# The last projection in four column strips, and a block that ends without GpSimd's drain

## Chip, cores, metric

The kernel runs on one core of one Trainium2 chip. The metric is the device time of one execution in microseconds (us). Executions of one kernel here spread over 0.2 to 0.7 us of 1329, and the change edits the last three microseconds. So the document uses two rulers. The timed runs say whether the whole became faster. The trace says what each step after the last load took; those steps repeat within about 0.01 us from look to look (a look is one profiled execution).

## The reference

Two decode attentions, A and B, each with one query token and 32 query heads of 128; their two outputs of 512 stand side by side.

```python
# A: 32 key/value heads, all 32768 keys.  B: 8 key/value heads, the last 4096 keys.
q = (x @ wq).reshape(B, Sq, H, Dh).transpose(0, 2, 1, 3)
scores = jnp.einsum("bhqd,bhkd->bhqk", q, k_cache) * (Dh ** -0.5)
p = softmax(scores)
o = jnp.einsum("bhqk,bhkd->bhqd", p, v_cache)
out = o.transpose(0, 2, 1, 3).reshape(B, Sq, H * Dh) @ wo      # [1,4096] @ [4096,512]
# ... result: concatenate([out_A, out_B], -1), bfloat16 [1, 1, 1024]
```

Nearly all bytes are A's keys and values: 2 x 32 x 32768 x 128 x 2 bytes = 537 MB of the 570 MB read.

## The kernel before

The kernel streams K and V through two large buffers. After the last head the weight `wo` of A comes in five pieces (`WO_CUTS`), each with its own semaphore, so that the projection follows the pieces as they land. A row of the result is a sum over 32 matmuls with one stationary column each. To use more of the PE array than one column, each matmul is split into two strips of 256 result columns; they go to different column groups of the array and to PSUM partitions 0 and 64, and run together (the two start 3 to 4 ns apart in the trace).

```python
    def build(self):
        nc = self.nc
        with nc.Block() as block:
            # ... plan the operations of each engine, then emit them

    WO_CUTS = {"A": (0, 11, 19, 25, 29, 32), "B": (0, 16, 32)}

    def plan(self):
        # ... all loads and both attentions; the loads of wo are issued last
        self.emit_spread("A")
        self.emit_proj()
        for n in ("B", "A"):
            self.op("sp", lambda e, n=n: e.wait_ge(self.outsem[n], 16))

    def proj_part(self, name, part, out):
        a0, a1 = self.WO_CUTS[name][part:part + 2]
        # ... one matmul group for each a in a0..a1, via `out`
        return self.op("pe", mm, (self.wosem[name][part], 16), self.c[name]["ozop"])

    def halves(self, e, bank, lhsT, rhs, begin, end):
        for i in range(2):
            inst = e.matmul(bank[64 * i:64 * i + 1, 0:256], lhsT=lhsT, rhs=rhs[:, 256 * i:256 * i + 256], start=begin,
                            stop=end, tile_position=(0, 64 * i), skip_group_check=True)
        return inst

    def store(self, name, bank, off, dep):
        c = slice(off // 2, off // 2 + 256)
        o = self.op("dve", lambda v: v.tensor_copy(self.out_sb[0:65, c], bank[0:65, 0:256]), dep)
        self.op("sp", lambda e: e.dma_start(self.out[0, :, off:off + 512].rearrange("a (i x) -> (a i) x", i=2),
                                            self.out_sb[0:65:64, c]).then_inc(self.outsem[name], 16), o)

    def emit_proj(self):
        # ... B: four strips of 512 over heads, copied to pb, summed by two halves into ACC
        self.store("B", self.ACC, 512, o)
        for part in range(len(self.WO_CUTS["A"]) - 1):
            o = self.proj_part("A", part, lambda e, lhsT, rhs, a: self.halves(e, self.PT, lhsT, rhs, a == 0, a == 31))
        self.store("A", self.PT, 0, o)
```

## Time and profile before

| | |
|---|---|
| Time, median of 3 runs | 1328.72 us (1328.62 to 1329.13) |
| Span in the profile | 1326.8 us |
| DMA | 430 GB/s over the span |
| Last piece of A's `wo` landed | 1323.81 us |

In the views, PE is TensorE's matmuls, PEld its weight loads, DVE VectorE, ACT ScalarE, POOL GpSimd and SP SyncE; a q marks an instruction of the engine's instruction queue. A load or store has landed when its semaphore is full. Lines of the page of the kernel before: span, the granted PE clock and the DMA busy share in 40 slices (tenths), and the chain that ended last, by engine.

```profile
span 1326.8 us, 28797 instructions
...
PEclk9877788887788888778888878888887888888798
DMA  9999999999999999999999999999999999999998
...
DMA 70%; PE 28%; DVE 1%; issue 0%; SPq 0%; ACT 0%
```

DMA is busy nine tenths or more in 39 slices of 40, and 70% of the chain is DMA. PE's clock in these slices of 33 us is an average. A change of the projection can therefore only gain where DMA has nothing left to do: after the last load.

The same chain in order of time, its last pieces (start, length, what). The DMA piece is the last load from its issue to its landing.

```profile
1290.58 33.23 DMA kbuf<-in_A_wo_dram
...
1323.85 0.51 PE psPT L655 x6
...
1324.39 0.42 DVE out_sb L661
```

The timeline of the end, without the weight loads (start, length, engine, line, operation, count; in brackets the idle time before it and what ended it):

```profile
1323.85 0.49 PE L655 MATMUL psPT<-kbuf,oz_A 128*1 128x256 bf16 x6 [0.34 <-DMA kbuf<-in_A_wo_dram]
1324.39 0.42 DVE L661 CAST out_sb<-psPT 65x256 bf16<-65x256 f32 x1 [5.65 <-PE psPT L655]
1324.84 0.49 SPq L662 DMA_DIRECT2D out_dram<-out_sb  x1
```

After the load: PE 0.51 us, VectorE's cast 0.42 us, SyncE's store. The store's semaphore was full at 1326.34, 1.50 us after its issue began. From there to the end of the span are 0.47 us. They are the block's end; the instructions of it on SyncE, and GpSimd's drain (line 94; duration, then first and last start):

```profile
L94 POOLq DRAIN  x1: 1817/1817/1817, 1.2 to 1.2; - x1
...
L94 SPq COMPARE_BRANCH  x1: 33/33/33, 1326.4 to 1326.4; - x1
L94 SPq DRAIN  x1: 7/7/7, 1326.6 to 1326.6; - x1
L94 SPq EVENT_SEMAPHORE  x1: 17/17/17, 1326.7 to 1326.7; - x1
```

GpSimd's drain starts at 1.2 us and lasts until 3.0, while GpSimd sets up its constants. SyncE goes through a branch and a drain at the end, then a barrier of all engines. The span ends at 1326.8; the device time is longer, after the program's end.

PE's busy time, the granted clock and the DMA share in the last three windows of the trace's clock record, 3.41 us each:

```profile
core 0: us, PE busy (x) PEld busy (x) DVE busy (x) ACT busy (x) POOL busy (x), PEclk, DMA share, GB/s
1316.56:1319.98 3.42, 2.26 (x38) 1.22 (x32) 1.11 (x2) 0.00 (x0) 0.00 (x0) 1.00 0.99 401
1319.98:1323.39 3.41, 2.19 (x36) 1.19 (x32) 0.00 (x0) 0.00 (x0) 0.00 (x0) 1.00 0.44 177
1323.39:1326.80 3.41, 0.61 (x10) 0.18 (x6) 0.42 (x1) 0.00 (x0) 0.00 (x0) 1.00 0.00 0
```

The clock is full (1.00) up to the last matmul; PE was busy 2.26 and 2.19 us of 3.41 in the two windows before the last load.

### The profile page before, as it was taken

What the parts mean: (1) busy time and instruction counts of PE and PEld (TensorE: products, weight loads), DVE (VectorE), ACT (ScalarE), POOL (GpSimd) and SP (SyncE); (2) the same over time, 40 slices, a digit from 0 to 9 for tenths busy, and PEclk for the clock granted to TensorE, in tenths of its full rate; (3) what the DMA queues carried; (4) which work ended last, traced back from release to release, by engine and by line L of the source; (5) the groups of instructions that cost most, each with busy time, mean ns of one, the idle gap of its engine ahead of it and who ended that gap; (6) DMA issues with size and microseconds to landing.
All of it is one profiled execution on the core that took longest, in us unless ns stands there. A gap on an engine that the chain in (4) does not pass through costs nothing.

```text
span 1326.8 us, 28797 instructions
## 1 busy us (share of the span) xinstructions
PE 964.5 (73%) x13436; PEld 679.5 (51%) x13436; DVE 749.8 (57%) x1345; ACT 54.8 (4%) x167; POOL 2.3 (0%) x17
## 2 busy tenths in 40 slices
PE   3757678777667877766787777678777767877786
PEld 3544455554445555444565544456554445655453
DVE  3645466665456666545666645566654556665473
ACT  0000000000000000000000000000000000000000
POOL 0000000000000000000000000000000000000000
PEclk9877788887788888778888878888887888888798
DMA  9999999999999999999999999999999999999998
GB/s 394 431 431 438 432 433 433 437 429 433 433 435 437 433 435 431 433 433 435 437 433 435 431 433 433 431 441 433 431 435 433 431 433 441 433 431 435 433 431 344
DMA packets 13079, 570.66 MB, mean 430 GB/s; under 512 B 1540, under 2 KB 1544, under 8 KB 1928
## 3 DMA queue, kind: packets, MB, share of 16 engines
q1 hardware_dynamic: 12776, 570.43, 99.6%
q8 instruction: 12, 0.20, 0.1%
q10 hardware_dynamic: 288, 0.00, 0.0%
q14 instruction: 3, 0.02, 0.0%
HBM read 570.43 MB, written 0.00 MB: 430 GB/s over the span
## 4 chain that ended last, share of the span: by engine, by line
DMA 70%; PE 28%; DVE 1%; issue 0%; SPq 0%; ACT 0%
DMA kbuf<-in_A_k_cache_dram 65%; PE psT L491 23%; PE psS L513 4%; DMA kbuf<-in_B_k_cache_dram 3%; DMA kbuf<-in_A_wo_dram 3%; DVE kt L494 1%; PE psACC L593 0%; SPq L286 0%; DVE oc_A L609 0%; ACT psb L541 0%; DVE tr_in L530 0%; PE psPT L565 0%; ACT ptsb L568 0%; PE psPT L655 0%; PE psG L620 0%
## 5 line engine op out<-in xcount | busy, mean ns | idle before, releaser
L494 DVE COPY kt<-psT 128x1024 bf16<-128x1024 bf16 x1056 | 655.2, 684 | 245.0 <-PE psT L491 243.1
L491 PE MATMUL psT<-ident,kbuf 128*128 128x128 bf16 x8448 | 579.2, 234 | 176.2 <-DMA kbuf<-in_A_k_cache_dram 164.4
L491 PEld LDWEIGHTS psT<-ident,kbuf 128*128 128x128 bf16 x8448 | 539.7, 106 | 268.2 <-DMA kbuf<-in_A_k_cache_dram 172.5
L593 PE MATMUL psACC<-vbuf,ptsb 128*4 128x512 bf16 (+1 forms) x2112 | 183.2, 523 | 23.1 <-ACT ptsb L568 21.3
L513 PE MATMUL psS<-kt,qw 128*32 128x512 bf16 x2048 | 157.6, 385 | 15.5 <-DVE kt L494 15.5
L607 DVE TENSOR_SCALAR oc_A<-psACC,hot_A 128x128 f32<-128x128 f32 x32 | 11.2, 351 | 247.8 <-PE psG L620 247.8
L593 PEld LDWEIGHTS psACC<-vbuf,ptsb 128*4 128x4 bf16 (+1 forms) x2112 | 60.0, 110 | 136.9 <-issue 87.2
L541 ACT ACTIVATE psb<-psS,nb_A 128x512 bf16<-128x512 f32 x32 | 22.0, 687 | 1169.9 <-DVE nb_A L540 1169.9
L513 PEld LDWEIGHTS psS<-kt,qw 128*32 128x32 bf16 x2048 | 34.0, 95 | 58.0 <-DVE kt L494 31.4
L620 PE MATMUL psG<-oc_A,hw 128*32 128x128 f32 (+1 forms) x128 | 19.3, 227 | 52.3 <-DVE oc_A L609 52.3
L620 PEld LDWEIGHTS psG<-oc_A,hw 128*32 128x32 f32 x128 | 11.4, 109 | 62.4 <-DVE oc_A L609 55.0
L565 PE MATMUL psPT<-ident,psb 128*128 128x128 bf16 x136 | 17.9, 274 | 34.0 <-ACT psb L541 34.0
L609 DVE SCALAR_TENSOR_TENSOR oc_A<-psACC,hot_A,oc_A 128x128 f32<-128x128 f32 x96 | 33.7, 351 | 3.4
L530 DVE TENSOR_REDUCE tr_in<-psS 128x1 f32<-128x512 f32 x34 | 23.5, 692 | 17.1 <-PE psS L513 17.1
L565 PEld LDWEIGHTS psPT<-ident,psb 128*128 128x128 bf16 x136 | 10.0, 116 | 37.0 <-ACT psb L541 36.7
L534 PE MATMUL psACC<-rows,tr_in 128*1 128x64 f32 x64 | 8.7, 217 | 25.6 <-DVE tr_in L530 25.6
L568 ACT ACTIVATE ptsb<-psPT 128x512 bf16<-128x512 bf16 x34 | 20.3, 597 | 28.2 <-PE psPT L565 28.2
L534 PEld LDWEIGHTS psACC<-rows,tr_in 128*1 128x1 f32 x64 | 2.7, 81 | 35.1 <-DVE tr_in L530 35.1
L538 PE MATMUL psACC<-mr_A,nscale 1*128 1x1 f32 x64 | 12.1, 256 | 9.8 <-DVE mr_A L537 9.8
L538 PEld LDWEIGHTS psACC<-mr_A,nscale 1*128 1x128 f32 x64 | 9.4, 183 | 15.7 <-DVE mr_A L537 15.7
L540 DVE COPY nb_A<-psACC 128x1 f32<-128x1 f32 x32 | 5.1, 158 | 15.0 <-PE psACC L538 15.0
L537 DVE TENSOR_REDUCE mr_A<-psACC 1x1 f32<-1x64 f32 x32 | 6.8, 213 | 11.7 <-PE psACC L534 11.7
(71 smaller groups left out, 75.1 us busy)
## 6 DMA issues: line engine op xcount, KB each, us to landing
kbuf<-in_B_k_cache_dram SPq DMA_DIRECT2D x2, 4096.0 KB, 32.5
vbuf<-in_B_v_cache_dram SPq DMA_DIRECT2D x2, 4096.0 KB, 23.6
kbuf<-in_A_k_cache_dram SPq DMA_DIRECT2D x2, 4096.0 KB, 22.0
vbuf<-in_B_wq_dram SPq DMA_DIRECT2D x1, 4096.0 KB, 12.3
vbuf<-in_A_wq_dram SPq DMA_DIRECT2D x1, 4096.0 KB, 32.4
kbuf<-in_B_wo_dram SPq DMA_DIRECT2D x2, 2048.0 KB, 33.1
kbuf<-in_A_wo_dram SPq DMA_DIRECT2D x1, 1408.0 KB, 28.5
kbuf<-in_A_wo_dram SPq DMA_DIRECT2D x1, 1024.0 KB, 30.6
```

Source lines behind the costliest of these rows:

```text
L491: inst = e.transpose(T[:, 128 * k:128 * k + 128], src[:, DH * k:DH * k + DH], self.ident[:, :])
L494: self.copies.append(self.op("dve", lambda v: v.tensor_copy(KT[:, :], T[:, :]), o, to="pe"))
L513: inst = e.matmul(self.S[32 * c:32 * c + 32, :], lhsT=win, rhs=self.kt[(bb + c // 2) % NKT][:, 512 * (c % 2):512 * (c % 2) + 512], start=b ...
L530: o = dve(lambda v: v.reduce_max(tr["in"][:, 0:1], self.S[:, :], axis=AXX), self.sdone, self.k_pool, to="pe" if name == "A" else None)
L534: o = self.op("pe", lambda e: e.matmul(self.ACC[0:1, 0:64], lhsT=tr["in"][:, 0:1], rhs=self.rows64[:, :], start=True, stop=True, skip_grou ...
L538: o = self.op("pe", lambda e: e.matmul(self.ACC[:, 64:65], lhsT=self.nscale[:, :], rhs=t["mr"][0:1, :], start=True, stop=True, skip_group_ ...
L541: self.sread = self.op("act", lambda s: s.activation(out=self.psb[:, :], in_=self.S[:, :], func=ACTF.Exp, bias=t["nb"][:, k:k + 1], scale= ...
L565: inst = e.transpose(PT[:, 128 * jj:128 * jj + 128], self.psb[:, 128 * jj:128 * jj + 128], self.ident[:, :])
L568: self.ptread = self.op("act", lambda s: s.activation(out=self.ptsb[:, :], in_=PT[:, 0:512], func=ACTF.Copy), self.psread, to="pe")
L593: inst = e.matmul(acc[32 * c:32 * c + rows, 0:512], lhsT=lhsT, rhs=rhs, start=begin, stop=end, tile_position=(0, 32 * c), skip_group_check ...
L609: o = self.op("dve", lambda v, src=src, hot=hot: v.scalar_tensor_tensor(out=oc, in0=src, scalar=hot, in1=oc, op0=ALU.mult, op1=ALU.add), p ...
L620: return self.op("pe", lambda e: e.matmul(self.G[0:32, c0 + c:c0 + c2], lhsT=win, rhs=t["oc"][g % 2][:, c:c2], start=False, stop=True, ski ...
```

## The change

Its intent: halve the columns of the last matmuls and of the copy that follow the last load, and spare GpSimd's drain at the end of the block. `no_gpsimd_drain` is an option of the block. The order of the two output semaphores changed as well.

```diff
-        with nc.Block() as block:
+        with nc.Block(no_gpsimd_drain=True) as block:
...
-        self.outsem = {n: s(f"outsem_{n}") for n in self.X}
+        self.outsem = {n: s(f"outsem_{n}") for n in ("B", "A")}
...
-    def halves(self, e, bank, lhsT, rhs, begin, end):
-        for i in range(2):
-            inst = e.matmul(bank[64 * i:64 * i + 1, 0:256], lhsT=lhsT, rhs=rhs[:, 256 * i:256 * i + 256], start=begin,
-                            stop=end, tile_position=(0, 64 * i), skip_group_check=True)
+    def strips(self, e, bank, lhsT, rhs, begin, end, parts):
+        w = 512 // parts
+        for i in range(parts):
+            r = 128 // parts * i
+            inst = e.matmul(bank[r:r + 1, 0:w], lhsT=lhsT, rhs=rhs[:, w * i:w * i + w], start=begin,
+                            stop=end, tile_position=(0, r), skip_group_check=True)
         return inst
-    def store(self, name, bank, off, dep):
-        c = slice(off // 2, off // 2 + 256)
-        ... cast of rows 0..64, store of rows 0 and 64
+    def store(self, name, bank, off, dep, parts):
+        w, step = 512 // parts, 128 // parts
+        rows, c = 128 - step + 1, slice(off // 2, off // 2 + w)
+        ... cast of rows 0..rows-1, store of every step-th row
...
-        self.store("B", self.ACC, 512, o)
+        self.store("B", self.ACC, 512, o, 2)
-            o = self.proj_part("A", part, lambda e, lhsT, rhs, a: self.halves(e, self.PT, lhsT, rhs, a == 0, a == 31))
-        self.store("A", self.PT, 0, o)
+            o = self.proj_part("A", part, lambda e, lhsT, rhs, a: self.strips(
+                e, self.PT, lhsT, rhs, a == 0, a == 31, 4))
+        self.store("A", self.PT, 0, o, 4)
```

## The prediction

> **What bounds the kernel now.** The page's DMA row reads 9 tenths in 39 of 40 slices, 430 GB/s over the span; PE is busy 73%, DVE 57%. The chain that ended last is 70% DMA. The change edits only the last three microseconds. From the timeline of the end, span 1326.8 us:
>
> - the last piece of A_wo lands at 1323.81 (the chain of waits: 33.2 us of DMA before it, then PE);
> - PE runs the last six one-row matmuls of 256 columns from 1323.85; the chain gives them 0.51 us (pairs 0.11 us apart, 0.27 us each);
> - DVE copies 65x256 to out_sb at 1324.39, 0.42 us;
> - SP issues the store at 1324.84 (0.49 us); it lands at about 1326.34;
> - SP then takes two waits and a branch, drains at 1326.59, and the block's barrier is over at 1326.8.
>
> So 3.0 us lie between the last load and the span's end; the measured time is 1.9 us longer, taken as constant.
>
> **What the change does, costed.**
>
> 1. Strips. 64 matmuls of 256 columns become 128 of 128. Pairs in different strips start 3 to 7 ns apart and run together; B's groups of four do so too (512 columns, 0.43 us at half clock). Only the last three rows' groups are exposed. Estimate at full clock: two steps of 0.055 us plus one matmul of 0.22 us and the semaphore, 0.36 instead of 0.51: -0.15 us. Earlier parts wait for DMA.
>  Risk: the matmuls fill less of the stretch before the last part, so the granted clock, 1.0 there, may fall to 0.5. The Trainium skill ("TensorE: Matmul & The Clock Gate", Part 1) puts the window at 3.4 us; the trace's clock record changes in such steps (1313.15, 1316.56). At half clock 128 columns take what 256 took, and the gain is zero. I weigh this at 40%: -0.09 us expected.
> 2. Copy. 97x128 instead of 65x256. Casts of 32 and 256 columns take 192 and 421 ns here; by that line 128 take 290: -0.13 us, all on the chain.
> 3. Store. Four rows of 256 B instead of two of 512 B. The Trainium skill ("DMA: Bandwidth & Descriptors", Specifications) says that transfers under 512 B are read, modified and written. No transfer of this trace shows it for a store; estimate +0.05 us, between 0 and +0.3.
> 4. Drain. GpSimd's own drain stands at 1.2 us and lasts 1.8 us, over 1300 us before the end; removing it saves nothing. Built, the other four engines' drain and arrival at the barrier become two instructions; SP's one is on the chain: about +0.03 us.
> 5. Order of the two output semaphores. Now the wait for the last store comes first and a branch carrying the other follows 0.07 us later; exchanged, the last wait sits on the branch: -0.06 us.
>  PE's program grows by 128 instructions; I expect the same one instruction fetch in the tail (1317.6 us).
>
> Sum: about -0.2 us of 1328.7, or 0.015%, below the 0.5 us between before's three runs.
>
> **Prediction:** 1328.5 us, 8 in 10 between 1327.9 and 1329.1. Faster by over 2%: 0.5%; within 2%: 99%; slower: 0.5%.
>
> **What would show each step right.** Same DMA row; last matmul group 0.36 us after its landing (1: 0.5 if the clock fell); the 97x128 cast near 290 ns (2); from the store's issue to its landing 1.5 us as before, or longer (3); from that landing to the end of the span 0.43 to 0.46 us (4, 5).
>
> **What would make it wrong.** A store of short rows that takes a microsecond longer; an extra instruction fetch that delays the last load or stalls PE; the time up to the last load shifting by itself.

## The result

Changed kernel: 1328.89 us, median of 5 runs (1328.79 to 1329.09). Kernel before, now 5 runs: 1329.06 us (1328.62 to 1329.18). All runs are fast (a slow one would lie over 1.5% above the fastest). The ratio is 1.0, with a 95% interval of 0.9988 to 1.0012. A ratio here is the mean time of one kernel's fast runs over that of the other's of the same rounds, so it is not quite the ratio of the medians: the medians differ by 0.17 us, the means by less than 0.01 us. Same.

The page after:

```profile
span 1326.8 us, 28928 instructions
...
DMA  9999999999999999999999999999999999999998
...
DMA 70%; PE 28%; DVE 1%; SPq 0%; issue 0%; ACT 0%
```

The end of the chain, and the timeline of the end without the weight loads:

```profile
1289.93 33.89 DMA kbuf<-in_A_wo_dram
...
1323.87 0.52 PE psPT L657 x7
...
1324.41 0.29 DVE out_sb L664
```

```profile
1323.87 0.49 PE L657 MATMUL psPT<-kbuf,oz_A 128*1 128x128 bf16 x12 [0.35 <-DMA kbuf<-in_A_wo_dram]
1324.41 0.29 DVE L664 CAST out_sb<-psPT 97x128 bf16<-97x128 f32 x1 [7.54 <-PE psPT L657]
1324.73 0.54 SPq L665 DMA_DIRECT2D out_dram<-out_sb  x1
```

The last load landed at 1323.82, within 0.02 us of before. The cast is shorter, 0.29 us. But PE's piece of the chain is 0.52 us, not 0.36, although each matmul has half the columns. The windows say why (columns as in the fence of before):

```profile
1312.17:1315.58 3.41, 2.22 (x36) 0.74 (x36) 1.20 (x4) 0.00 (x0) 0.00 (x0) 1.00 1.00 420
1315.58:1319.00 3.42, 1.38 (x48) 0.69 (x48) 0.59 (x2) 0.00 (x0) 0.00 (x0) 1.00 0.99 404
1319.00:1322.41 3.41, 1.72 (x56) 1.25 (x56) 0.00 (x0) 0.00 (x0) 0.00 (x0) 0.50 0.68 275
1322.41:1325.82 3.41, 1.20 (x35) 0.51 (x28) 0.29 (x1) 0.00 (x0) 0.00 (x0) 0.50 0.06 23
```

In 1315.58 to 1319.00 PE was busy 1.38 us, at full clock. In the next two windows the clock is 0.50, and the last matmuls run in them. The groups of four are 0.107 us apart after the second (the first two stand 0.06 apart), which is what pairs of 256 columns took before.

The instructions of the block's end on SyncE:

```profile
L94 SPq EVENT_SEMAPHORE  x2: 17/17/17, 1326.6 to 1326.8; - x2
...
L94 SPq COMPARE_BRANCH  x1: 38/38/38, 1326.4 to 1326.4; - x1
L94 SPq DRAIN  x1: 7/7/7, 1326.6 to 1326.6; - x1
```

GpSimd's drain is gone from the list. SyncE has two semaphore instructions instead of one: its drain no longer reports to the barrier itself, an instruction at 1326.62, 0.06 us after the drain, does.

The steps after the last load, in two looks at each kernel, read from the trace's instructions and semaphore updates (us; a landing is the last update of a load's or store's semaphore). The second looks, before2 and after2, are experiments of the next section.

| Look | clock at the last group | last load landed | landing to cast | cast | store, issue | store, issue to landing | landing to span's end | sum, last load to end |
|---|---|---|---|---|---|---|---|---|
| before | 1.0 | 1323.81 | 0.58 | 0.421 | 0.49 | 1.500 | 0.466 | 2.99 |
| before2 | 1.0 | 1324.25 | 0.58 | 0.421 | 0.49 | 1.496 | 0.460 | 2.98 |
| after | 0.5 | 1323.82 | 0.59 | 0.292 | 0.54 | 1.585 | 0.536 | 3.03 |
| after2 | 0.5 | 1323.89 | 0.59 | 0.290 | 0.54 | 1.590 | 0.535 | 3.03 |

So the end did not shrink by 0.2 us; it grew by 0.03 to 0.05. Of three steps that should have paid, one paid. Between the cast's end and the store's issue lie 0.03 us in each.

### The profile page after: what moved, and what is told of

Same layout as the page of the kernel before. It is cut to its first block, busy times and chain, and to the rows that moved or that the text cites. A ratio compares the mean times of both kernels' runs of the same rounds, so it can differ in the third digit from the quotient of the medians.

```text
span 1326.8 us, 28928 instructions
## 1 busy us (share of the span) xinstructions
PE 962.3 (73%) x13500; PEld 677.7 (51%) x13500; DVE 749.5 (56%) x1345; ACT 54.8 (4%) x167; POOL 2.3 (0%) x17
## 4 chain that ended last, share of the span: by engine, by line
DMA 70%; PE 28%; DVE 1%; SPq 0%; issue 0%; ACT 0%
DMA kbuf<-in_A_k_cache_dram 65%; PE psT L491 23%; PE psS L513 4%; DMA kbuf<-in_B_k_cache_dram 3%; DMA kbuf<-in_A_wo_dram 3%; DVE kt L494 1%; PE psACC L593 0%; SPq L286 0%; DVE oc_A L609 0%; ACT psb L541 0%; PE psPT L565 0%; DVE tr_in L530 0%; ACT ptsb L568 0%; PE psPT L657 0%; PE psG L620 0%
```

## The experiments

Theory A: the strips leave PE idle while it waits for DMA, so the granted clock falls to half before the last part. Rivals: B, the clock windows begin at a random place, and the fall was chance; C, groups of strips cannot follow one another faster whatever the clock, because of the weight loads between them. For the end of the block the theory is that the option splits an instruction on SyncE's path; the rival is that the store or the exchanged semaphores lengthen it. Single looks are of unknown state (one run each); they are used for the lengths of steps, not for total times. Each was correct.

### before2: the kernel before, again

Edit: none.

> The kernel before, unchanged, a second look. Question: is the granted clock in the last 3.4 us before the last load lands a matter of the kernel or of chance? Theory A (the strips make PE too idle, the clock falls): the clock is full (1.0) at 1323 us here again, and the last matmul group takes about 0.51 us from its first matmul to its semaphore, pairs 0.11 us apart. Theory B (the clock windows start at a random place, the fall was chance): the clock may be half here, and then the pairs are 0.21 us apart and the group takes about 0.75 us. Both: cast 0.42 us, store from issue to landing 1.5 us, from landing to the end of the span 0.47 us.

Measured: clock 1.0, pairs 0.108 to 0.109 us apart, PE from first matmul to semaphore 0.511 us, cast 0.421, store 1.496, end 0.460. That fits A, and B is not yet excluded: the windows began at nearly the same place as in the first look (1316.47 against 1316.56). The last load landed 0.43 us later than in the first look of the same kernel, more than the change was to gain.

### after2: the changed kernel, again

Edit: none.

> The changed kernel, unchanged, a second look. Theory A: half clock (0.5) in the last two parts again, groups of four strips 0.107 us apart, last group 0.52 us. Theory B: full clock in about half of such looks, groups 0.056 us apart, last group 0.36 us. Both: cast 0.29 us, store from issue to landing 1.58 us, from landing to the end of the span 0.54 us.

Measured: clock 0.5, the last group as in the first look (0.518 us). The windows began elsewhere:

```profile
1314.52:1317.94 3.42, 1.66 (x56) 0.64 (x52) 1.11 (x2) 0.00 (x0) 0.00 (x0) 1.00 0.99 407
1317.94:1321.35 3.41, 0.88 (x52) 0.50 (x40) 0.00 (x0) 0.00 (x0) 0.00 (x0) 1.00 0.87 352
1321.35:1324.76 3.41, 1.89 (x52) 1.03 (x52) 0.29 (x1) 0.00 (x0) 0.00 (x0) 0.50 0.17 68
```

The clock stayed full through a window with 1.66 us of PE work and fell after one with 0.88 us, 1317.94 to 1321.35. That window holds the wait for two of the load pieces.

### nodrain_only: the kernel before with the block's end changed alone

```diff
-        with nc.Block() as block:
+        with nc.Block(no_gpsimd_drain=True) as block:
```

> The kernel before with the block's end changed alone. If splitting drain and barrier arrival into two instructions is what lengthened the end: from the landing of the last store to the end of the span 0.53 to 0.54 us, against 0.47 before; SyncE's drain is followed by a semaphore instruction 0.06 us later. If the longer end came from the four-row store or the exchanged semaphores: 0.47 us. All else as before: cast 0.42 us, store 1.50 us from issue to landing.

Measured: from the store's landing to the end 0.535 us, against 0.466 and 0.460 before; the cast (0.421) and store (1.498) as before. SyncE's end shows the added instruction, as in the changed kernel:

```profile
L94 SPq EVENT_SEMAPHORE  x2: 17/17/17, 1326.6 to 1326.7; - x2
...
L94 SPq DRAIN  x1: 7/7/7, 1326.5 to 1326.5; - x1
```

So the option alone costs 0.07 us here; the rival falls. The same look also tells A from B. Its clock windows begin where after2's did, within 0.1 us, and it has two strips:

```profile
1314.45:1317.86 3.41, 1.66 (x28) 0.58 (x18) 1.11 (x2) 0.00 (x0) 0.00 (x0) 1.00 1.00 413
1317.86:1321.27 3.41, 1.80 (x31) 0.99 (x26) 0.00 (x0) 0.00 (x0) 0.00 (x0) 1.00 0.89 357
1321.27:1324.69 3.42, 1.91 (x26) 0.87 (x26) 0.36 (x1) 0.00 (x0) 0.00 (x0) 1.00 0.18 72
```

PE was busy 1.66 and 1.80 us in the windows where after2 had 1.66 and 0.88, and the clock stayed full. At the same place of the windows, two strips keep the clock and four strips lose it. B falls. Two strips are no guarantee: in rows_apart, below, the clock fell at 1313.52 after a window with 1.63 us of PE work and came back at 1320.34. It was full at the last group in all five looks at two strips.

### warm: the changed kernel with PE kept busy

```diff
+    def filler(self, n):     # n matmuls of 128x512 into an unused PSUM bank
+        ...
         strips = ...                       # B's copy to pb runs on VectorE
+        self.filler(3)
         ...                                # B's last matmuls
+        self.filler(3)
         for part in range(5):
             o = self.proj_part("A", part, ...)
+            if self.FILL[part]: self.filler(self.FILL[part])      # FILL = (6, 4, 2, 1, 0)
```

> The changed kernel with filler matmuls (128x512, results unused) in PE's waits for the last projection's parts, so that PE stays busy. Theory A: the clock stays at 1.0 to the end of the last group, the groups stand 0.056 us apart and the last one takes 0.36 us instead of 0.52; span shorter by 0.15 us if the last load lands at the same time after the start. Rival C (four strips cannot run faster than 0.107 us a group whatever the clock, because of the weight loads of 0.08 to 0.13 us between them): clock 1.0, but groups still 0.107 us apart and 0.5 us in all.

Measured: the clock is full to the end. PE busy and clock in the last two windows, then the last group and the cast:

```profile
1318.24:1321.65 3.41, 2.89 (x42) 1.13 (x40) 0.00 (x0) 0.00 (x0) 0.00 (x0) 1.00 0.86 345
1321.65:1325.06 3.41, 2.10 (x55) 0.89 (x55) 0.29 (x1) 0.00 (x0) 0.00 (x0) 1.00 0.16 59
```

```profile
1323.89 0.34 PE L657 MATMUL psPT<-kbuf,oz_A 128*1 128x128 bf16 x12 [0.23 <-DMA kbuf<-in_A_wo_dram]
1324.28 0.29 DVE L664 CAST out_sb<-psPT 97x128 bf16<-97x128 f32 x1 [7.40 <-PE psPT L657]
```

The groups stand 0.055 us apart, first matmul to semaphore 0.368 us, landing to cast 0.435 instead of 0.586. C falls: the same instructions run twice as fast at full clock. A stands, and the gain of the strips over the kernel before is 0.14 us once the clock is held (0.579 to 0.435). Last load to end: 2.88 us.

### waits_swapped: the order of the two final waits

```diff
-        for n in ("B", "A"):
+        for n in ("A", "B"):
             self.op("sp", lambda e, n=n: e.wait_ge(self.outsem[n], 16))
```

> The changed kernel with the two final waits written in the other order, so that the compiled program waits for the first store (B) alone and for the last store (A) on the branch. If a separate wait ahead of the branch costs its step: from the landing of the last store to the end of the span 0.47 us instead of 0.54. If the branch itself is what takes the 0.07 us: unchanged, 0.54.

Measured: landing to end 0.470 us instead of 0.536. SyncE's separate wait (line 395) ran at 1326.3 in the changed kernel, after the last landing; here it is over long before it:

```profile
L395 SPq EVENT_SEMAPHORE  x1: 17/17/17, 1325.4 to 1325.4; - x1
```

In the program, the wait that is written first ends up on the branch, and the other on an instruction ahead of it. Before and after, that other one waited for store A, the last to land, and the branch came 0.066 us later. The change exchanged the numbers of the semaphores, not the order of the waits: the built program lists them in the same order in both kernels. This look was at half clock too, after a window with 1.12 us of PE work.

### one_strip: one strip, one row

```diff
-                e, self.PT, lhsT, rhs, a == 0, a == 31, 4))
-        self.store("A", self.PT, 0, o, 4)
+                e, self.PT, lhsT, rhs, a == 0, a == 31, 1))
+        self.store("A", self.PT, 0, o, 1)
```

with `out_sb` widened to 1024 columns, so that A's row does not meet B's.

> The changed kernel with the last projection in one strip: matmuls of 512 columns, a cast of 1x512, a store of one row of 1024 B. It gives a third point for each step beside 2 and 4 strips. PE is busier, so the clock should be full: last group 2 x 0.216 + 0.38 = 0.81 us. Cast by the line through 128, 256 and earlier copies of 512 columns: 0.68 to 0.69 us. Store: if the issue takes longer by the row (0.488 at two, 0.54 at four, 0.026 a row), 0.46 us for one; from issue to landing, if the rows or engines count, 1.45 us; if short rows below 512 B were what made the four-row store longer, 1.50 us less the 0.026 of the issue, so also near 1.47, and the two are then not told apart by this run.

Measured: the cast 0.678 us, as expected. PE missed by far: landing to cast 1.71 us, not about 0.9. The expectation had PE idle at the landing, but 32 matmuls of 512 columns take 7.07 us, one after the other, and PE was behind the loads:

```profile
1318.42 7.07 PE L657 MATMUL psPT<-kbuf,oz_A 128*1 128x512 bf16 x32
...
1325.52 0.68 DVE L664 CAST out_sb<-psPT 1x512 bf16<-1x512 f32 x1 [6.47 <-PE psPT L657]
```

So it takes at least two strips for PE to follow the loads. The store missed too, and in the interesting direction: issue 0.282 us, issue to landing 1.144, against 0.488 and 1.500 for two rows and 0.540 and 1.585 for four. Neither explanation in the expectation foresaw that step.

### rows_apart: the kernel before, its last store as two stores of one row

```diff
-        self.op("sp", lambda e: e.dma_start(<rows 0 and 64, 2 x 512 B>).then_inc(self.outsem[name], 16), o)
+        for i in range(2):
+            self.op("sp", lambda e, i=i: e.dma_start(<row 64 * i, 512 B>).then_inc(self.outsem[name], 16), o)
```

and the wait for A's semaphore at 32.

> The kernel before with its last store written as two stores of one row of 512 B each, one after the other on SyncE's queue. The one-row store of one_strip was issued in 0.28 us and landed 1.14 us after its issue began, the two-row one in 0.49 and 1.50. If a second row in one store costs the difference (0.36 us) and a store of its own is cheap: the second store begins about 0.3 us after the first and lands 1.44 us after the first began, a little sooner than 1.50. If the 512 B size matters (one_strip's row had 1024 B): each of the two lands later than 1.14 us after its own issue, and the sum is above 1.50. Else as before: cast 0.42 us, landing to end 0.47 us.

Measured, taking the landings in the order of the issues: the first store landed 1.12 us after its issue began, the second 1.08 us after its own; the second began 0.335 us after the first. In all 1.42 us, against 1.50 for both rows in one store. A row of 512 B takes what a row of 1024 B took (1.14), so the size within this range is not the cost; several rows in one store are. Where a second row's 0.36 us go, the trace's DMA packets tell. From the begin of the issue to the first packet of data, a store of one row took 0.76 us (one_strip, and the first store here), of two rows 1.13 (before), of four 1.19 (after); from that packet to the landing it was 0.36 to 0.41 us in all of them. So the second row costs before any data moves, 0.2 us of it in the issue on SyncE. Why it does is not settled.

### two_queues: one row each on SyncE's and ScalarE's queue

```diff
-        self.store("A", self.PT, 0, o)
+        # last matmul of each strip signals its own engine
+        # VectorE casts row 0,  SyncE stores it;  ScalarE casts row 64, ScalarE's queue stores it
...
-        for n in ("B", "A"):
+        for n in ("A", "B"):                 # A's semaphore to 32
```

> The kernel before (two strips, GpSimd's drain kept) with the two result rows handled apart: VectorE copies row 0 and SyncE stores it, ScalarE copies row 64 and its queue stores it, and the wait for these stores sits on the branch. If a one-row store costs 1.14 us whatever queue issues it: last load to cast 0.58, cast 0.42 on both engines or a little more on ScalarE, store 1.14, landing to end 0.39, in all 2.56 us from the last landing to the end of the span, against 2.74 in best and 2.99 before. If the two stores hinder one another or ScalarE's issue is slow: 2.7 to 3.0. Timed: 0.4 us or 0.03% at most, not resolved, verdict same.

Measured: 2.71 us from the last load to the end, not 2.56. The casts ran together (0.41 and 0.38 us), and the issues began together:

```profile
1324.26 0.41 DVE L686 CAST out_sb<-psPT 1x256 bf16<-1x256 f32 x1 [5.72 <-PE psPT L656]
1324.29 0.38 ACT L688 ACTIVATE out_a<-psPT 1x256 bf16<-1x256 f32 x1 [20.26 <-PE psPT L662]
1324.69 0.51 ACTq L691 DMA_DIRECT2D out_dram<-out_a  x1
1324.70 0.28 SPq L691 DMA_DIRECT2D out_dram<-out_sb  x1
```

ScalarE's issue took 0.51 us, SyncE's 0.28. The two landings came 1.12 and 1.31 us after the issues began. The two share a semaphore, but the trace's DMA packets carry their queue: ScalarE's row moved 0.76 us after its issue began, as a single row on SyncE's queue did, and SyncE's 0.78 us. So ScalarE's longer issue did not delay its row. In one_strip and rows_apart the landing followed a row's packet by 0.36 to 0.39 us; here the first landing came 0.36 us after ScalarE's packet and the second 0.52 us after SyncE's. The 0.15 us missed were lost after both rows had moved, while the two stores were ending together; why stays open. Timed: 1328.82 us (1328.45 to 1328.91, 5 runs) against 1328.88 (1328.63 to 1329.24, 9 runs) before; ratio 1.0, 0.9986 to 1.0013. Same.

### best: strips, clock held, drain kept, waits swapped

Edit: warm, plus `nc.Block()` as before, plus the edit of waits_swapped.

> Four strips, filler matmuls that hold the clock, GpSimd's drain kept, and the last store's wait put on the branch. By the steps measured so far: last load to cast 0.435, cast 0.29, issue to landing 1.59, landing to end 0.40, in all 2.74 us from the last load's landing to the end of the span, against 2.99 in the kernel before and 3.03 in the changed one. Timed, that is 0.25 us of 1328.9, or 0.02%, and is expected to stay below what the rounds resolve: verdict same.

Measured: every step as expected; 2.736 us from the last load to the end (0.435 + 0.292 + 0.03 + 1.587 + 0.394), against 2.99 before. Timed: 1328.51 us (1328.39 to 1328.60, 5 runs) against 1328.87 us (1328.60 to 1329.34, 9 runs) of the kernel before in the same rounds; ratio 0.9997, interval 0.9983 to 1.001. 0.03% is not resolved by the rounds. The five runs do lie at or below the fastest of the nine, and their spans, 1326.5 to 1326.7 us, below all nine of before, 1326.9 to 1327.5. That is more than the 0.25 us of the steps; whether the rest is the last load's landing, which the table shows to wander, is not shown. Its clock windows begin within 0.03 us of those of waits_swapped (1316.07 and 1316.09), and there, at four strips without fillers, the clock fell; here it held to 1326.31. That is a second pair at one place of the windows.

### best_cut: the last load piece cut once more

```diff
-    WO_CUTS = {"A": (0, 11, 19, 25, 29, 32), ...
+    WO_CUTS = {"A": (0, 11, 19, 25, 29, 31, 32), ...
```

on top of best, with no filler before the last part.

> As best, with the last load cut from three rows a partition to two and one, so that only one group of strips follows the last landing. If PE's part is what the groups sum to: last load to cast 0.33 us instead of 0.435, in all 2.63 us. The last landing itself may come up to 0.1 us later or earlier for the extra, smaller transfer. Timed: same.

Measured: landing to cast 0.324 us and 2.63 us in all, as expected. The last load landed at 1323.96, 0.10 us later than in best, and the profiled span is the same, 1326.6 us. Timed: 1328.67 us (1328.54 to 1328.84), ratio 0.9998, same. Looks of one kernel differ in that landing by more (before: 1323.81 and 1324.25), so whether the extra transfer caused the 0.10 us is open.

## Why the prediction was right or wrong

The time was inside the range: 1328.89 us, forecast 1328.5, between 1327.9 and 1329.1. "Same" at 2% was right for the reason given: DMA bounds the kernel (430 GB/s before and after), and the change works on 3 us of 1329. That the time fell into the range says nothing of the five steps: three of the five runs of the unchanged kernel lie in it too, and the other two within 0.1 us of it. The sum of about -0.2 us was not what happened. In the trace the end grew by 0.03 to 0.05 us.

1. *Strips, -0.15 us at full clock, -0.09 expected.* Measured +0.01. The named risk came true: the clock fell to half in every look at four strips without fillers (after, after2, waits_swapped). The mechanism was right, its weight was not: 40% was too low, since after2 against nodrain_only shows that the fall follows from the strips. At held clock (warm) the step gave 0.14 us and 0.368 us for the last group, nearly as costed.
2. *Copy, -0.13 us.* Right: 0.421 to 0.292 us. The line through casts of 32 and 256 columns gave 0.290; one_strip's 512 columns took 0.678.
3. *Store, +0.05 us.* The sign was right, the size was low: +0.085. The reason was wrong or at least not shown. Of the 0.085, 0.05 is a longer issue on SyncE. The experiments show a cost of rows, not of short rows: one row 1.14 us at 1024 B and 1.12 at 512 B, two rows 1.50, four rows 1.59. Four rows of 512 B were not tried. But the packets leave little room for a dear short row: one of 256 B took 15 ns (after), one of 512 B 25 (before), one of 1024 B 44 (one_strip), and from the first packet to the landing four rows took 0.40 us against 0.37 for two.
4. *Drain, +0.03 us.* The sign was right, the size low: +0.07, shown by nodrain_only. Removing GpSimd's drain gained nothing, since it ran at 1.2 us.
5. *Exchanged semaphores, -0.06 us.* Wrong: no effect. I read the wait order in the trace as the order of the semaphore numbers. It is the order in which the program writes the waits, and the change left that alone. waits_swapped gives the 0.066 us that the prediction had ascribed to the exchange.

The sum: +0.01 - 0.13 + 0.085 + 0.07 + 0 = +0.035 us, which is within the +0.03 to +0.05 of the table. The 0.17 us between the medians is not part of it: the last load lands anywhere between 1323.69 and 1324.25 from look to look, and that alone moves the time by more. What sets that landing was not studied.

"TensorE: Matmul & The Clock Gate" in the Trainium skill (Part 1) gives the window as about 3.4 us and the clocks as half and full; the trace agrees, its clock record has only 0.5 and 1.0 and steps of 3.41 us. Part 3 of the page counts about 4 ns of issue overhead for each tile that is packed into the array, column tiles included; at full clock the strips of a last group start 2 to 4 ns apart. "DMA: Bandwidth & Descriptors" (Why a DMA increments its semaphore by 16 and not by 1) says that only the DMA engines in use report, and that the issuing sequencer writes the rest at once. The trace agrees: the last store's semaphore has 2 updates for one row, 3 for two and 5 for four, and the first comes before any data has moved (1325.74 against 1325.97 in before), though 0.42 us after the issue ended.

## What to carry to other kernels

Where TensorE waits for DMA, making its work smaller can cost it its clock; then look at the granted clock of the window before the step on the chain, and at how many columns stream in it. When only the last microseconds are free, add up the steps after the last load from the trace and test each one alone; these timed runs could not tell a change of 0.02%. An option that removes a wait may add an instruction to another engine's path, so read the built program's end, including on which instruction each wait sits.

## What the Trainium skill lacked or had wrong

- "TensorE: Matmul & The Clock Gate", Part 1, says that the clock falls after an idle window, and its section "Why this matters for your kernels" asks for no idle gaps above about 3 us. Neither is enough. In the changed kernel PE's longest gap in the stretch in which the clock fell was 1.71 us. In these runs the share of work in a window decides, for which the page has no number: near the end the clock fell after windows in which PE was busy 0.88, 1.12, 1.27 (kernel before, from 1309.73) and 1.38 us of 3.41, and held after 1.80 and 2.19 us (busy by the trace's modelled ends, at full clock). Busy time is not the measure itself: between 1.62 and 1.86 us it went both ways (1.66 held in after2, 1.86 fell in best_cut from 1310.86), and after 3.41 us of 3.41, mostly one-column matmuls, it fell (before, from 36.56). The time in which columns stream fits better. Estimated from the matmul starts of all twelve traces, with 0.216 us for 512 columns (one_strip's spacing) and overlapping strips counted once, 788 of 789 whole windows at full clock that a fall followed have at most 1.08 us of it, and 2231 of 2233 that none followed have more.
- The same page, Part 2, gives about 81 ns a matmul for streams of weight load and matmul with 128 columns. That is no figure for column strips, whose packing Part 3 measures at 512 columns: with four column strips and one-column weights (warm) groups of four stood 55 ns apart, 14 ns a matmul.
- "DMA: Bandwidth & Descriptors" gives no cost for the number of rows in a small store. Issue, and issue to landing: one row 0.28 and 1.14 us, two rows 0.49 and 1.50, four rows 0.54 and 1.59. Nor does it say that issue time may differ by engine: a one-row store of 512 B took 0.28 us on SyncE and 0.51 us on ScalarE (two_queues).
- The same page, Specifications, names a read-modify-write below 512 B. No run here shows it: the four-row store of 256 B rows took 0.03 us more than the two-row store of 512 B rows after its issue ended, and the number of rows changed with the size; its data packets took 15 ns each, those of 512 B 25 ns.
- No page has the end of a block: without GpSimd's drain the other engines' drain and barrier arrival become two instructions, 0.07 us on SyncE's path; and a separate wait ahead of the branch costs 0.066 us.
